# Shifted ranks, a planned transfer queue and another order at the end, in a kernel whose order a planner writes

## The chip, the cores and the metric

The kernel runs on one core of a Trainium2 chip. A core has five engines that run their own instruction lists and meet through semaphores: TensorE (PE, matrix products; its weight loads are listed as PEld), VectorE (DVE), ScalarE (ACT), GpSimd (POOL) and SyncE (SP), which here does nothing but issue transfers (DMAs). SBUF is the on-chip memory; PSUM, in eight banks of 128 partitions x 512 floats, takes the results of TensorE. The metric is the time of one execution in microseconds (us) on the device, as the median of several runs; lower is better.

## What is computed

Two attention layers over 2048 tokens of width 512, side by side in one output. Cut to what matters:

```python
def A(x, wq, wk, wv, wo):                      # 32 query heads of 16, one shared key/value head
    q = heads(x @ wq); k = x @ wk; v = x @ wv
    p = softmax(einsum("bhqd,bkd->bhqk", q, k) / 4)
    return merge(einsum("bhqk,bkd->bhqd", p, v)) @ wo

def B(x, wqkv, w_phi, wo):                     # linear attention with a feature map
    q, k, v = heads(x @ wqkv)
    phi = lambda t: concat(softmax(t @ w_phi), softmax(-(t @ w_phi)))
    kv = einsum("bhsf,bhsd->bhfd", phi(k), v); z = phi(k).sum(over tokens)
    return merge(phi(q) @ kv / (phi(q) @ z + 1e-6)) @ wo

return concat([A(...), B(...)], axis=-1)
```

Nearly all work is in A: 32 heads x 2048 x 2048 exponentials, 134 million. B needs no pairwise scores.

## The kernel before, in words

**Units.** The scores of A are cut into 32 stages (`sc`; 512 queries of one group of four heads), each of 16 quads (one key block of 128 by the four heads of a group), each quad of four units: one matrix product with 32 rows of contraction (L1611) that fills one PSUM bank with 128 x 512 scores. That makes 512 quads and 2048 units.

**Two ways to an exponential.** Most quads go to ScalarE: `next_qk` gathers three units and then two, in turn, into banks 0 to 2 and 3 to 4, and `expo` (L1672) takes the exponential of all of them in one instruction into the ring `PT` of 20 slots. The others go to VectorE: `next_dq` puts one unit at a time into a free bank, `bits` (L1782) turns scores into half-precision bit patterns by one multiply and add with integer output, and after four units `shift` (L1795) makes three shifted copies; TensorE adds up the four copies with fitting weights (L1828), which gives a close approximation of the exponential. A quad on VectorE takes four L1782 and three L1795. Which quad goes where isn't fixed: VectorE takes one whenever the planner finds it free enough (`dq_ok`, `dve_quad`).

**Sums.** The exponentials times the values, and the row sums beside them, accumulate in bank 5 (`ACC`), by L1726 for quads from ScalarE and L1828 for those from VectorE. When all 16 quads of a stage are in, `finish_sc` copies the bank out (`accS`, L1426), and the row sums go a long way: a transfer lays them out over partitions (`denC`, L1852, four transfers), VectorE takes reciprocals (L1860), four transfers bring them back to a row (L1865) and four spread the row over 16 partitions (`denS`, L1871), and `finish_sc3` multiplies (L1878). Odd stages are written to `Od` and moved into `On` by four more transfers (L1884). After every eight stages `outproj` makes four output blocks, copied to `outA` (ring of two) and stored (L1907). In the last stage the row sums have a bank of their own (`den_bank`), filled in the same steps as `ACC`, and `finish_last` computes reciprocals on ScalarE as exp(-ln) (L1926, L1928), multiplies on VectorE (L1932), adds the last quarter of the output projection (L1936) to what `out_part` (L1917, jobs `pp`) has put into four banks, copies (L1944 and L1426) and stores (L1946): blocks 0 and 2 issued by ScalarE, blocks 1 and 3 by SyncE. Part B's work is woven in between (`jobs_b`): projections L2042, L2072 and L2133, exponentials L2050 and L2140, products L2150 and L2186, and VectorE work on them.

**The planner.** None of this order is written out. Each piece is a job with an engine, an assumed duration, the jobs it comes after, the number of PSUM banks it needs (0 to 4 belong to ScalarE's scores, 6 and 7 are the free ones) and a rank, `prio`, where less is sooner. `run` plays the machine forward in a model of its own time: for every engine it lists the jobs that may start, keeps those within 0.02 us of the earliest, takes the one with the least `rank`, and issues it. The order in which jobs are issued is the order of the instruction lists that the engines get; on the chip each engine follows its list and waits on semaphores. `tr` and `tw` hold when the model thinks a tile was last read and written. A batch of transfers (`dmas`) is given a fixed time from its producer's end to its landing, whatever else stands on SyncE.

**Fillers.** TensorE's clock is kept up with products that add zero (`fill`, L1420, and `company`, L1403). `put_fill` and `short` place them where the planner reckons too little activity; they need a bank: `ACC` while a stage is open, otherwise a free one, otherwise the first bank of the next scores.

## Time and profile before

| | us |
|---|---|
| median of 3 runs (lowest, highest) | 769.65 (767.93, 771.23) |
| the profiled execution | 767.89 |
| its span, first to last instruction | 765.8 |
| ScalarE busy | 742.8 (97%) |
| PE busy | 716.3 (94%) |
| VectorE busy | 712.0 (93%) |
| mean granted clock of TensorE | 0.995 of full |

Rows of groups read: line, engine, operation, output<-inputs, shapes, count | busy us, mean ns of one | idle time of the engine before them and what ended it. Rows of a timeline: start, duration, engine, line, operation, tiles, count, and in brackets the idle time before. SPq and ACTq are the sequencers of SyncE and ScalarE issuing transfers. Rows of stretches: from:to, length, busy time of each engine with its count of instructions, granted clock, share of the transfer engines, GB/s. Busy time of ScalarE and VectorE counts the union of overlapping instructions, so a pause shorter than the overlap isn't seen in it.

Of the kernel before, what the change touches and what calls it, by code (L numbers as in the profile page):

```python
# [1169 lines left out]
class _Fast:  # L1170
# [16 lines left out]
    def __init__(self, nc, st, ins, out):  # L1187
# [75 lines left out]
        self.last_full = 0.0  # L1263

# [246 lines left out]
    def jobs_a(self):  # L1511
        ps, xT, job = self.ps, self.xT, self.job
# [200 lines left out]
    def pv(self, q):  # L1713

        ps, PT, VA = self.ps, self.PT, self.VA
        sc, kap = self.aquads[q]
        slots = [(4 * q + g) % self.RING for g in range(4)]
        todo = [(self.ACC, VA[:, sc % 2, kap, :], self.sums(sc))]
        if sc == 31:
            d = self.dens()  # L1720
            todo.append((self.den_bank, self.ones[:, 0:32], d))
        for bank, w, (start, stop) in todo:
            def fn(pe, bank=bank, w=w, start=start, stop=stop):
                mm = None
                for g in range(4):
                    mm = pe.matmul(ps[32 * g:32 * g + 32, bank, :], lhsT=w, rhs=PT[:, slots[g], :], start=start, stop=stop, tile_position=(0, 32 * g))  # L1726
# [115 lines left out]
    def finish_sc(self, sc):  # L1842

        ps = self.ps
        r = sc % 2
        accS, denC = self.accS, self.denC
        self.copy(accS[:, r, :], ps[:, self.ACC, :], [("PS", self.ACC)], [("accS", r)])
        fs = []
        for g in range(4):
            src = accS[32 * g + 16 - 16 * r:32 * g + 17 - 16 * r, r, :].rearrange("p (b c) -> p b c", b=32)  # L1850
            dst = denC[32 * g:32 * g + 32, r, :]
            fs.append((lambda s_, d_: (lambda q: q.dma_start(d_, s_)))(src, dst))  # L1852
        self.dmas(fs, [("accS", r)], [("denC", r)], 4.4)
        if self.rec is None:
            self.acc_sc = sc + 1

    def finish_sc2(self, sc):
        r = sc % 2
        denC, R = self.denC, self.denS
        self.add("dve", lambda v: v.reciprocal(out=denC[:, r, :], in_=denC[:, r, :]), reads=[("denC", r)], writes=[("denR", r), ("denC", r)])  # L1860
        fs = []
# [4 lines left out]
        self.dmas(fs, [("denR", r)], [("row", r), ("denS", r)], 4.4)  # L1866
# [5 lines left out]
        self.dmas(fs, [("row", r)], [("denS", r)], 11.0)  # L1872

    def finish_sc3(self, sc):
# [5 lines left out]
        if r:  # L1880
# [4 lines left out]
            self.dmas(fs, [key], [("On", sl)], 5.0)  # L1885
# [15 lines left out]
    def outproj2(self, qt):  # L1901
# [5 lines left out]
        self.dmas([lambda q: q.dma_start(dst, oa[:, ring, :])], [("outA", ring)], [], 4.0, is_output=True)  # L1907


    def out_part(self, i):  # L1910
        ps, On = self.ps, self.On
        bank = self.bank(("pp", i))

        def fn(pe):
            mm = None
            for A in range(4):
                mm = pe.matmul(ps[:, bank, :], lhsT=On[:, A, i * 128:i * 128 + 128], rhs=self.wo2[:, A, :], start=(A == 0), stop=False)  # L1917
            return mm
        self.add("pe", fn, reads=[("On", A) for A in range(4)] + ["wo2"], writes=[("PS", bank)])

    def finish_last(self):
# [8 lines left out]
        for h in range(2):  # L1930
# [3 lines left out]
            for i in range(2 * h, 2 * h + 2):  # L1934
                bank = self.bank(("pp", i))
                self.add("pe", (lambda i, bank: (lambda pe: pe.matmul(ps[:, bank, :], lhsT=Od[:, 1, i * 128:i * 128 + 128], rhs=self.wo2[:, 3, :], start=False, stop=True)))(i, bank),  # L1936
                         reads=[("Onl", h), "wo2"], accum=[("PS", bank)])
        for i in range(4):
            bank = self.bank(("pp", i))
# [5 lines left out]
            dst = self.out[0, (12 + i) * 128:(13 + i) * 128, 0:512]  # L1945
            self.S.dma1((lambda o, dst: (lambda q: q.dma_start(dst, o)))(o, dst), reads=[key], queue="sp" if i % 2 else "act", is_output=True)  # L1946

    def flag_calc(self):
# [7 lines left out]
        self.dmas([lambda q: q.dma_start(self.mrow, mqk)], [("mqk", k) for k in range(4)], ["mrow", "Bwv"], 8.0)  # L1956
# [273 lines left out]
    def b_s8c(self, st):  # L2230
# [3 lines left out]
        self.dmas([lambda e: e.dma_start(dst, ob[:, st % 3, :])], [("outB", st % 3)], [], 4.0, is_output=True)  # L2234
# [11 lines left out]
    FORCE = 3.3  # L2246
    LAST = 6
# [22 lines left out]
    def run(self):  # L2270
        while True:
            picks = []
            for eng, c in self.cand.items():
# [11 lines left out]
                now = [o for o in opts if o[0] <= lo + 0.02]  # L2285
# [7 lines left out]
            bank = self.ACC if self.open else next((b for b in self.free if self.tr.get(("PS", b), (0.0,))[0] + self.SEM <= self.te["pe"]), None)  # L2293
# [21 lines left out]
    def put_fill(self, n, m, bank, te):  # L2315
        cols = [512] * (n // 4) + ([128 * (n % 4)] if n % 4 else [])
        start = bank != self.ACC
# [11 lines left out]

    def rank(self, o):  # L2330

        s, j = o
        p = j.prio
        if j.eng == "pe":
# [95 lines left out]
```

### The profile page before, as it was taken

The numbers are of one execution on the slowest core, as the hardware profiler recorded it, in microseconds if no ns is written. First come the engines' busy times: TensorE is split into PE (matmuls) and PEld (weight loads), VectorE is DVE, ScalarE is ACT, GpSimd is POOL, SyncE is SP. The second block draws the span as 40 slices with busy tenths as digits, with TensorE's granted clock in tenths as the row PEclk, the third lists the DMA queues.
The fourth block names the chain that finished last, engine by engine and source line by source line (L and its number), as shares of the span: only waits on it lengthen the run. The fifth ranks groups of instructions, "written<-read, shape, count | busy, mean of one in ns | idle before, by whom it ended". The sixth has DMA issues, their size and how long they took to land.

```text
span 765.8 us, 17760 instructions
## 1 busy us (share of the span) xinstructions
PE 716.3 (94%) x7536; PEld 240.5 (31%) x7596; DVE 712.0 (93%) x1242; ACT 742.8 (97%) x694; POOL 18.5 (2%) x73
## 2 busy tenths in 40 slices
PE   7999999999998999999999999999999999999997
PEld 3332333233332333333332332223333333333222
DVE  3999999999998998799999999999997999999991
ACT  5999999999999999999999999999998999999996
POOL 6000000000000002000000000000000000000000
PEclk9999999999999999999999999999998999999999
DMA  9911011111012101110111110112111011111102
GB/s 183 206 9 8 6 8 13 8 10 12 1 12 36 9 6 8 13 9 16 19 9 19 16 15 14 15 11 30 22 20 8 20 28 25 23 15 12 10 8 38
DMA packets 47521, 18.15 MB, mean 24 GB/s; under 512 B 38468, under 2 KB 45572, under 8 KB 47432
## 3 DMA queue, kind: packets, MB, share of 16 engines
q1 hardware_dynamic: 44920, 16.47, 16.6%
q8 instruction: 61, 1.00, 0.5%
q10 hardware_dynamic: 2512, 0.44, 0.4%
q14 instruction: 28, 0.23, 0.1%
HBM read 2.15 MB, written 4.19 MB: 8 GB/s over the span
## 4 chain that ended last, share of the span: by engine, by line
ACT 73%; DVE 12%; PE 11%; DMA 2%; SPq 1%; issue 0%; ACTq 0%
ACT f_PT L1672 70%; DVE f_Z L1782 4%; PE f_ps L1611 3%; DVE f_Z L1795 3%; PE f_ps L1828 2%; ACT f_ET L2140 2%; PE f_ps L1726 2%; ACT f_Ek L2050 1%; DVE f_ssum L2056 1%; DMA f_AxT<-in_A_x_dram 1%; DVE f_vS L2082 1%; DVE f_Wk L2196 1%; PE f_ps L1420 1%; PE f_ps L1403 0%; PE f_ps L1917 0%
## 5 line engine op out<-in xcount | busy, mean ns | idle before, releaser
L1672 ACT ACTIVATE f_PT<-f_ps 128x1536 bf16<-128x1536 f32 x623 | 716.3, 1311 | 14.9 <-DVE f_VK L1581 8.2
L1782 DVE TENSOR_SCALAR f_Z<-f_ps 128x512 int16<-128x512 f32 x492 | 320.7, 680 | 17.4 <-PE f_ps L1611 15.8
L1611 PE MATMUL f_ps<-f_QA,f_KR 32*128 32x512 bf16 x2048 | 314.7, 385 | 23.2 <-ACT f_PT L1672 11.2
L1795 DVE TENSOR_SCALAR f_Z<-f_Z 128x2048 int16<-128x2048 int16 x369 | 243.0, 684 | 0.4
L1611 PEld LDWEIGHTS f_ps<-f_QA,f_KR 32*128 32x128 bf16 x2048 | 81.7, 91 | 237.7 <-ACT f_PT L1672 134.5
L1726 PE MATMUL f_ps<-f_PT,f_VA 128*32 128x512 bf16 x1556 | 153.5, 391 | 2.2 <-DVE f_accS L1426 1.8
L1828 PE MATMUL f_ps<-f_Z,f_VK 128*32 128x512 f16 x1968 | 129.5, 383 | 1.1 <-DVE f_accS L1426 0.4
L1726 PEld LDWEIGHTS f_ps<-f_PT,f_VA 128*32 128x32 bf16 x1556 | 38.7, 93 | 98.9 <-issue 88.3
L1420 PE MATMUL f_ps<-f_ones,f_zero 128*128 128x512 bf16 (+10 forms) x372 | 66.2, 345 | 3.0 <-POOL f_zero L1438 1.3
L1828 PEld LDWEIGHTS f_ps<-f_Z,f_VK 128*32 128x32 bf16 x1968 | 42.4, 96 | 56.9 <-issue 12.6
L1403 PE MATMUL f_ps<-f_ones,f_zero 32*128 32x512 bf16 x144 | 49.4, 380 | 0.3
L1420 PEld LDWEIGHTS f_ps<-f_ones,f_zero 128*32 128x32 bf16 (+2 forms) x372 | 19.1, 97 | 32.7 <-issue 21.9
L2196 DVE TENSOR_TENSOR f_Wk<-f_ps,f_wq 128x512 bf16<-128x512 f32 x32 | 21.8, 683 | 0.0
L1426 DVE COPY f_accS<-f_ps 128x512 f32<-128x512 f32 x31 | 21.3, 686 | 0.1
L2140 ACT ACTIVATE f_ET<-f_ps 128x512 bf16<-128x512 f32 x32 | 20.1, 772 | 0.0
L2082 DVE TENSOR_TENSOR f_vS<-f_ps,f_rs 128x1024 bf16<-128x1024 f32 x16 | 19.5, 1219 | 0.0
L2056 DVE TENSOR_REDUCE f_ssum<-f_Ek 128x64 f32<-128x1024 bf16 x16 | 19.3, 1208 | 0.1
L2050 ACT ACTIVATE f_Ek<-f_ps 128x512 bf16<-128x512 f32 x32 | 19.3, 721 | 0.0
L2072 PE MATMUL f_ps<-f_Bwv,f_BxT 128*128 128x512 bf16 x53 | 14.3, 380 | 2.8 <-DVE f_outA L1426 1.2
L2133 PE MATMUL f_ps<-f_BxT,f_Wq 128*128 128x512 bf16 x54 | 14.5, 380 | 2.0 <-issue 1.2
L2042 PE MATMUL f_ps<-f_Wk,f_BxT 128*128 128x512 bf16 x57 | 15.0, 381 | 1.4 <-issue 0.6
L1403 PEld LDWEIGHTS f_ps<-f_ones,f_zero 32*128 32x128 bf16 x144 | 11.4, 92 | 15.1 <-issue 11.4
(100 smaller groups left out, 320.6 us busy)
## 6 DMA issues: line engine op xcount, KB each, us to landing
f_denS<-f_denS SPq DMA_DIRECT2D x124, 30.0 KB, 3.1
out_dram<-f_outB SPq DMA_DIRECT2D x16, 128.0 KB, 2.7
f_denC<-f_accS SPq DMA_DIRECT2D x124, 2.0 KB, 1.7
f_denS<-f_denC SPq DMA_DIRECT2D x124, 2.0 KB, 1.7
out_dram<-f_outA SPq DMA_DIRECT2D x14, 128.0 KB, 2.1
f_On<-f_Od SPq DMA_DIRECT2D x60, 16.0 KB, 1.8
f_Bwv<-in_B_wqkv_dram SPq DMA_DIRECT2D x1, 512.0 KB, 4.7
f_Bwo<-in_B_wo_dram SPq DMA_DIRECT2D x1, 512.0 KB, 5.3
```

The lines of the kernel that those rows point to most:

```text
L1403: self.add("pe", lambda pe: pe.matmul(out, lhsT=zero[0:32, :], rhs=rhs, start=False, stop=False, tile_position=(0, 0)), reads=["ones", "ze ...
L1420: mm = pe.matmul(ps[x:x + m, bank, 0:n].rearrange("p (a n) -> p a n", n=128), lhsT=zero[0:r, 0:m], rhs=rhs, start=start, stop=start, **kw)
L1611: return pe.matmul(self.ps[:, bank, :], lhsT=self.KR[32 * g:32 * g + 32, sc % 2, kap * 128:(kap + 1) * 128], rhs=self.QA[32 * g:32 * g + 3 ...
L1672: self.add("act", lambda a: a.activation(out=PT[:, sl[0]:sl[0] + size, :], in_=ps[:, b0:b0 + size, :], func=ACT.Exp), reads=[("PS", b0 + i ...
L1726: mm = pe.matmul(ps[32 * g:32 * g + 32, bank, :], lhsT=w, rhs=PT[:, slots[g], :], start=start, stop=stop, tile_position=(0, 32 * g))
L1782: self.add("dve", lambda v: v.tensor_scalar(out=o, in0=ps[:, bank, :], scalar1=self.Z1, scalar2=self.Z0, op0=ALU.mult, op1=ALU.add), reads ...
L1795: self.add("dve", lambda v: v.tensor_scalar(out=Z[:, t], in0=Z[:, 0], scalar1=256.0 * t, scalar2=None, op0=ALU.add), reads=zk, writes=[("Z ...
L1828: mm = pe.matmul(ps[32 * g:32 * g + 32, bank, :], lhsT=w[:, k, :], rhs=Zf[:, k, sl[g], :], start=start and k == 0, stop=stop and k == 3, t ...
L2050: self.add("act", (lambda a, sg: (lambda e: e.activation(out=Ek[:, r, a].rearrange("p h f -> p (h f)"), in_=ps[:, bank, :], func=ACT.Exp, ...
L2082: self.add("dve", lambda v: v.tensor_tensor(out=vS[:, :, :, 0:16], in0=v3, in1=rs.unsqueeze(3).to_broadcast([128, 2, 32, 16]), op=ALU.mult ...
L2140: self.add("act", lambda e: e.activation(out=self.ET[:, sl, :], in_=self.ps[:, bank, :], func=ACT.Exp, scale=sg), reads=[("PS", bank)], wr ...
L2196: self.add("dve", lambda v: v.tensor_tensor(out=o, in0=i, in1=w.unsqueeze(3).to_broadcast([128, 16, 2, 16]), op=ALU.mult), reads=[("PS", b ...
```

## The change

Three things are changed, and none of the arithmetic.

1. *Ranks.* The model's time is cut into stretches of 20 us. Each has a number in `SEEDS` (38 numbers, ten of them 0). Where it isn't 0, every job's rank is shifted by up to half a unit either way, by a checksum of the number and the job's name, and the number modulo 4 chooses how late a job may start and still compete (0.02, 0.02, 0.06 or 0.12 us).
2. *Transfers.* `dmas` models SyncE as one queue (`spq`): a batch starts when the queue has come free, its producer has ended and what it reads has landed, takes 0.64 us per transfer, and lands a given time later. The given times are smaller than before in exchange. Fillers may also use `ACC` between two stages.
3. *The end.* `out_part` is cut into four jobs of one product each, ranked behind the sums, and the first of them may start while the last exponentials run, once the row sums of the last stage have their bank, only one free bank is left and part B needs none. In the last stage `den_bank` is filled before `ACC`. All four last stores are issued by SyncE, after all four copies.

```diff
@@ dmas
+        self.spq = max([self.spq, self.fin + 0.05] + [self.tw[r][0] + 0.1 for r in reads if r in self.tw]) + 0.64 * len(fs)
+        end = self.spq + us
         for r in reads:
-            self.tr[r] = max(self.tr.get(r, (0.0, "sp")), (self.fin + us, "sp"))
+            self.tr[r] = max(self.tr.get(r, (0.0, "sp")), (end, "sp"))
         for w in writes:
-            self.tw[w] = (self.fin + us, "sp")
+            self.tw[w] = (end, "sp")
@@ jobs_a
-            job(("pp", i), "pe", 0.87, (lambda i: (lambda: self.out_part(i)))(i), mode="full", nb=1, prio=2.0, ok=lambda: self.ended,
-                after=[("on", 24 + a) for a in range(7)])
+            for A in range(4):
+                job(("pp", i, A), "pe", 0.22, (lambda i, A: (lambda: self.out_part(i, A)))(i, A), mode="full", nb=0 if A else 1, prio=4.0,
+                    ok=lambda: self.asc >= 32 and self.dn % 4 == 0 and (self.ended or (self.den_bank is not None and len(self.free) == 1 and not self.rest_b())),
+                    after=[("pp", i, A - 1)] if A else [("on", 24 + a) for a in range(7)])
@@ pv
-        for bank, w, (start, stop) in todo:
+        for bank, w, (start, stop) in todo[::-1]:
@@ finish_sc, finish_sc2, finish_sc3, outproj2, b_s8c: landing times
-        self.dmas(fs, [("accS", r)], [("denC", r)], 4.4)
+        self.dmas(fs, [("accS", r)], [("denC", r)], 1.8)
-        self.dmas(fs, [("denR", r)], [("row", r), ("denS", r)], 4.4)
+        self.dmas(fs, [("denR", r)], [("row", r), ("denS", r)], 1.8)
-        self.dmas(fs, [("row", r)], [("denS", r)], 11.0)
+        self.dmas(fs, [("row", r)], [("denS", r)], 4.0)
-            self.dmas(fs, [key], [("On", sl)], 5.0)
+            self.dmas(fs, [key], [("On", sl)], 1.9)
-        self.dmas([lambda q: q.dma_start(dst, oa[:, ring, :])], [("outA", ring)], [], 4.0, is_output=True)
+        self.dmas([lambda q: q.dma_start(dst, oa[:, ring, :])], [("outA", ring)], [], 2.0, is_output=True)
...
@@ out_part
-    def out_part(self, i):
+    def rest_b(self):
+        return any(j.nb and j.name[0] not in ("pp", "dq") for c in (self.cand["pe"], [w for ws in self.waiting.values() for w in ws]) for j in c)
+
+    def out_part(self, i, A):
...
+        kw = dict(accum=[("PS", bank)]) if A else dict(writes=[("PS", bank)])
+        self.add("pe", lambda pe: pe.matmul(ps[:, bank, :], lhsT=On[:, A, i * 128:i * 128 + 128], rhs=self.wo2[:, A, :], start=(A == 0), stop=False),
+                 reads=[("On", A), "wo2"], **kw)
@@ finish_last
-            self.S.dma1((lambda o, dst: (lambda q: q.dma_start(dst, o)))(o, dst), reads=[key], queue="sp" if i % 2 else "act", is_output=True)
+            outs.append((o, key, self.out[0, (12 + i) * 128:(13 + i) * 128, 0:512]))
+        for i in (0, 1, 2, 3):
+            o, key, dst = outs[i]
+            self.S.dma1((lambda o, dst: (lambda q: q.dma_start(dst, o)))(o, dst), reads=[key], is_output=True)
@@ class constants
+    SEG = 20.0
+    JITTER = 1.0
+    SEEDS = (596854, 729634, 32076, 399722, 242082, 0, 0, 0, 0, 323517, 1029782, 888628, 860342,
+             597688, 434556, 856097, 34036, 281692, 360021, 0, 0, 231316, 0, 984916, 944571, 0,
+             641864, 18972, 805256, 0, 267693, 1039384, 154486, 560249, 867978, 713965, 845664, 0)
@@ run
-                now = [o for o in opts if o[0] <= lo + 0.02]
+                seed = self.seed(lo)
+                now = [o for o in opts if o[0] <= lo + (0.02, 0.02, 0.06, 0.12)[seed % 4]]
...
-            bank = self.ACC if self.open else next((b for b in self.free if self.tr.get(("PS", b), (0.0,))[0] + self.SEM <= self.te["pe"]), None)
+            bank = self.ACC if self.open else next((b for b in self.free + ([self.ACC] if self.acc_sc is not None and self.ndone[self.acc_sc] == 0 else [])
+                                                    if self.tr.get(("PS", b), (0.0,))[0] + self.SEM <= self.te["pe"]), None)
@@ rank
+        seed = self.seed(s)
+        if seed:
+            p += self.JITTER * (zlib.crc32(("%d%s" % (seed, j.name)).encode()) / 4294967296.0 - 0.5)
```

More of the change, by code (lines that the diff above doesn't have):

```diff
@@ L1 @@
+import zlib
 import contextlib
@@ L1263, in __init__ @@
         self.last_full = 0.0
+        self.spq = 30.0
     TAIL = dict(pe=0.17, act=0.15, dve=0.085, pool=0.1)
@@ L2316, in put_fill @@
         cols = [512] * (n // 4) + ([128 * (n % 4)] if n % 4 else [])
-        start = bank != self.ACC
+        start = bank != self.ACC or not self.open
         self.issue(_Job(("fill", len(self.log)), "pe", 0.0533 * n, lambda: self.fill(cols, start=start, mode=m, bank=bank), (), m, 0, (), 0, 9, None), te)
@@ L2328, in short, with seed @@
         return a + own < self.FORCE
+    def seed(self, t):
+        i = int(t / self.SEG)
+        return self.SEEDS[i] if i < len(self.SEEDS) else 0
     def rank(self, o):
```

18 lines of the change are left out of this document (6 added, 12 removed).

## The prediction

> **What bounds the kernel now.** I read the page first: busy time of each engine, then the costliest groups.
>
> ```profile
> span 765.8 us, 17760 instructions
> PE 716.3 (94%) x7536; PEld 240.5 (31%) x7596; DVE 712.0 (93%) x1242; ACT 742.8 (97%) x694; POOL 18.5 (2%) x73
> ...
> ACT 73%; DVE 12%; PE 11%; DMA 2%; SPq 1%; issue 0%; ACTq 0%
> ...
> L1672 ACT ACTIVATE f_PT<-f_ps 128x1536 bf16<-128x1536 f32 x623 | 716.3, 1311 | 14.9 <-DVE f_VK L1581 8.2
> L1782 DVE TENSOR_SCALAR f_Z<-f_ps 128x512 int16<-128x512 f32 x492 | 320.7, 680 | 17.4 <-PE f_ps L1611 15.8
> L1795 DVE TENSOR_SCALAR f_Z<-f_Z 128x2048 int16<-128x2048 int16 x369 | 243.0, 684 | 0.4
> L1726 PE MATMUL f_ps<-f_PT,f_VA 128*32 128x512 bf16 x1556 | 153.5, 391 | 2.2 <-DVE f_accS L1426 1.8
> ```
>
> ScalarE is the bound, with the chain of waits lying on its exponential (L1672) for most of the span; VectorE is almost as full. The two share one pool of work. There are 2048 score units of 512 columns; VectorE takes 492 of them (L1782) in groups of four, 123 quads, and ScalarE the other 1556 (the count of L1726). So an idle microsecond on either engine is worth something: on ScalarE directly, on VectorE if the planner fills it with a quad. By these rows a quad costs VectorE 4 x 320.7/492 + 3 x 243.0/369 = 4.58 us, and takes 4 x 716.3/1556 = 1.84 us off ScalarE. That ratio, 0.40 us of ScalarE for one of VectorE, prices most of what follows.
>
> Next I cut the span into stretches, to see where either engine is idle.
>
> ```profile
> core 0: us, PE busy (x) PEld busy (x) DVE busy (x) ACT busy (x) POOL busy (x), PEclk, DMA share, GB/s
> 20.00:240.00 220.00, 207.31 (x2223) 67.98 (x2240) 217.78 (x379) 219.84 (x210) 1.18 (x5) 1.00 0.18 25
> 240.00:254.00 14.00, 11.26 (x118) 3.51 (x119) 10.53 (x18) 11.71 (x11) 0.00 (x0) 1.00 0.20 43
> 254.00:580.00 326.00, 307.21 (x3266) 106.20 (x3296) 313.69 (x541) 325.52 (x310) 4.20 (x10) 1.00 0.13 15
> 580.00:592.00 12.00, 11.80 (x123) 3.85 (x127) 7.71 (x16) 8.92 (x8) 0.00 (x0) 0.72 0.12 8
> 592.00:736.00 144.00, 138.22 (x1400) 45.01 (x1399) 141.90 (x245) 143.45 (x128) 0.00 (x0) 1.00 0.15 19
> 736.00:756.00 20.00, 19.61 (x250) 5.69 (x248) 9.74 (x20) 19.73 (x19) 0.00 (x0) 1.00 0.14 12
> 756.00:766.00 10.00, 4.82 (x27) 1.71 (x26) 2.26 (x4) 2.68 (x6) 0.00 (x0) 0.98 0.17 57
> ...
> 300.00:320.00 20.00, 18.96 (x194) 6.67 (x196) 14.38 (x27) 20.00 (x23) 2.62 (x7) 1.00 0.12 8
> 500.00:520.00 20.00, 18.91 (x175) 6.23 (x177) 17.87 (x31) 20.00 (x22) 0.00 (x0) 1.00 0.13 17
> ```
>
> In the three quiet stretches, 690 us together, ScalarE is idle only 0.16 + 0.48 + 0.55 = 1.19 us and VectorE 2.22 + 12.31 + 2.10 = 16.63. Two holes stand out: at 240 to 254 ScalarE loses 2.29 us and VectorE 3.47, at 580 to 592 they lose 3.08 and 4.29. From 756 the tail runs off with every engine mostly idle. So the change has five places to pay in, and nothing of tens of microseconds.
>
> **Term 1, the transfer queue in the plan (the hole at 240).** Timelines of SyncE, VectorE and ScalarE:
>
> ```profile
> 237.08 3.35 SPq L1871 DMA_DIRECT2D f_denS<-f_denS  x4
> 240.47 6.23 SPq L1907 DMA_DIRECT2D out_dram<-f_outA  x4
> 243.28 0.69 DVE L1426 CAST f_outA<-f_ps 128x512 bf16<-128x512 f32 x1 [3.58 <-DMA out_dram<-f_outA]
> 245.43 1.02 ACT L1672 ACTIVATE f_PT<-f_ps 128x1024 bf16<-128x1024 f32 x1 [0.79 <-PE f_ps L1611]
> ```
>
> An output store stood on SyncE behind four spreads of the reciprocals, so its buffer came free late; VectorE stood 3.58 us before the copy that needed the buffer, and behind that copy the banks, the scores and the exponential went dry. The old plan gave each batch a fixed time from its producer; the new one gives 0.64 us per transfer on one queue, behind earlier batches, plus a landing time. For a batch met alone the sums are the old ones (4 x 0.64 + 1.8 = 4.36 against 4.4), so only collisions like this one change, and here VectorE would get other work first. No device wait is added. I take ScalarE's whole 2.29 us: **-2.3** (ends 0 and -3.6, VectorE's own wait). What is late next is the store itself, which nobody reads.
>
> **Term 2, the halved clock (the hole at 580).**
>
> ```profile
> 578.00:581.40 3.40, 2.43 (x21) 0.72 (x17) 3.40 (x7) 2.92 (x4) 0.00 (x0) 0.99 0.02 1
> 581.40:588.20 6.80, 6.71 (x57) 1.88 (x57) 3.90 (x8) 4.42 (x4) 0.00 (x0) 0.50 0.03 4
> 579.53 0.84 PE L1420 MATMUL f_ps<-f_ones,f_zero 128*128 128x512 bf16 x2 [0.79 <-ACT f_PT L1672]
> ```
>
> TensorE was busy 2.43 of 3.40 us, then got half the clock for 6.8 us; this is the one such event between start and tail. The filler at L1420 that should keep TensorE active waited 0.79 us for a bank that ScalarE still read. The change lets fillers use the accumulator bank between two stages once it has been copied out, and every changed rank rearranges the order. Each event is a coincidence of this order; with one in 745 us, none is about as likely as one, and the extra bank tips it. I take the hole as gone: **-3.1** (ends 0 and -3.4, half of 6.8). If an event stays, this term and its share of term 3 go.
>
> The Trainium skill ("TensorE: Matmul & The Clock Gate", section "HAM oscillation — how this bites in real kernels") gives as its abstract rule no gaps of TensorE over about 3.4 us. The rows above differ: the clock fell after a gap of 0.79 us. By that rule fillers that come a little sooner would be beside the point, and with term 2 and its share of term 3 at nothing the sum would be -7.2 instead of -12.0.
>
> **Term 3, quads for the VectorE time that terms 1 and 2 free.** 3.47 + 4.29 = 7.76 us, over 4.58, is 1.69 quads; times 1.84: **-3.1** (ends 0, if nothing is taken up, and -3.7 for two whole quads).
>
> **Term 4, the shifted ranks.** Every job's rank moves by up to half a unit, in 28 of 38 stretches of 20 us, and jobs up to 0.12 us later compete. Ten entries are 0 and leave the order alone. Host arithmetic costs the chip nothing. The trace can't show the new order, so bounds. Gain: all 16.63 us of quiet VectorE idle becomes quads, 3.63 x 1.84 = 6.7. Loss: the mean of quiet idle is 0.48 us in 20; if every shifted stretch became like 500 to 520 (2.13), 28 x 1.65 = 46 us, 10 quads, +18.5. Between these I go by one stretch, 300 to 320, with 5.62 us of the idle:
>
> ```profile
> 303.29 1.04 PE L2133 MATMUL f_ps<-f_BxT,f_Wq 128*128 128x512 bf16 x4 [0.26 <-ACT f_ET L2140]
> 310.33 0.69 DVE L1782 TENSOR_SCALAR f_Z<-f_ps 128x512 int16<-128x512 f32 x1 [1.87 <-PE f_ps L1611]
> ```
>
> VectorE waits there for scores (L1611) from a TensorE that runs full-size projections (L2133), and the ranks among just those jobs are what is shifted. I take that stretch mended and the rest as it is, 5.62/4.58 x 1.84 = 2.26: **-2.2**.
>
> **Term 5, the end.** Timelines of TensorE, ScalarE, VectorE and the queues:
>
> ```profile
> 755.90 0.81 PE L1917 MATMUL f_ps<-f_wo,f_On 128*128 128x512 bf16 x3 [0.16 <-issue]
> 756.64 0.40 PE L1726 MATMUL f_ps<-f_PT,f_VA 128*32 128x512 bf16 x4
> 756.87 0.39 PE L1726 MATMUL f_ps<-f_PT,f_ones 128*32 128x512 bf16 x4
> 757.19 2.76 PE L1917 MATMUL f_ps<-f_wo,f_On 128*128 128x512 bf16 x12
> 757.31 0.38 ACT L1926 ACTIVATE f_ET<-f_ps 128x256 f32<-128x256 f32 x1 [1.48 <-PE f_ps L1726]
> 758.17 0.48 DVE L1932 SCALAR_TENSOR_TENSOR f_Od<-f_ps,f_odd,f_ET 128x256 bf16<-128x256 f32 x1 [6.67 <-ACT f_ET L1928]
> 759.79 1.03 PE L1936 MATMUL f_ps<-f_wo,f_Od 128*128 128x512 bf16 x4
> 760.90 0.38 ACTq L1946 DMA_DIRECT2D out_dram<-f_outB  x1
> 761.22 2.36 SPq L1946 DMA_DIRECT2D out_dram<-f_outA  x2
> 761.38 0.60 ACT L1944 ACTIVATE f_outB<-f_ps 128x512 bf16<-128x512 f32 x1 [0.51 <-ACT f_outB L1944]
> 233.50 2.44 SPq L1865 DMA_DIRECT2D f_denS<-f_denC  x4
> ```
>
> The last sums (L1726) wait behind a projection of four matmuls; cut into single ones with a lower rank, they let the sums go 0.7 us sooner, and with the denominators' bank first another 0.2 (756.87 against 756.64): the logarithm starts 0.9 us earlier. The last projections (L1936) also wait for the twelve matmuls of L1917, until 759.79, though their first input is there at 758.65. One of the four banks may now be filled while the last exponentials run; the other three still go in the last two microseconds. So L1936 starts at best 0.9 us before 758.65, at 757.75, which is 2.0 before 759.79; the logarithm's 0.9 alone is the lower end of the gain. Against it: four stores on SyncE instead of two. At 0.61 us each (2.44 over 4) the last store may stand one issue longer, up to +0.6; in return ScalarE's second copy no longer waits 0.51 behind ScalarE's own store. Store 3 now stands behind store 2 and so behind ScalarE's second copy, which ends before VectorE's. I take **-1.3** (ends +0.6 and -2.0).
>
> **The sum.** -2.3 - 3.1 - 3.1 - 2.2 - 1.3 = -12.0 us. The profiled execution took 767.89 us, its span 765.8 and 2.1 around it; it becomes 755.9. The median of the runs, 769.65, is 1.76 above it, so I predict **757.6**.
>
> **Rivals.**
> - *The clock halves once in the new order as well.* For it: TensorE was busy for 2.43 of 3.40 us before the event, no rare thing once the order is another; against it the other 745 us of this order. Price: term 2 and the 4.29 us in term 3, 4.29 x 0.40 = 1.7: 757.6 + 3.1 + 1.7 = **762.4**. The Trainium skill's rule on gaps, above, leads to the same time.
> - *The gain is much larger*: all quiet VectorE idle goes. For it: 254 to 580 has 12.31 us of it in a few lumps. Against: VectorE also needs free banks and TensorE. 757.6 - 6.7 + 2.2 = **753.1**, and with the far ends of terms 1, 2, 3 and 5 another 2.9: 750.2.
> - *The plan moves and the chip doesn't*: holes of the old size open elsewhere, and term 4 is nothing; only term 5 is left: **768.4**. For it: unloaded transfers are priced as before.
> - *Slower, by starved VectorE*: shifted ranks put full-size projections ahead of VectorE's scores, as at 300 to 320. Each such stretch costs 5.62 less 0.48, 5.14 x 0.40 = 2.1 us. Without term 4 the sum is -9.8; it comes out 0.5% slower (+3.85) from 13.65/2.1, seven such stretches of 28; with eight: 769.65 - 9.8 + 16.8 = **776.7**. Against it: in before there is one in 35 quiet ones.
>
> **Chances.** My forecast 0.43 (753 to 761), larger gain 0.15, clock event 0.20, only the end 0.12, starved 0.10. The first three are faster by over 0.5%, about what a measurement here can tell from no change (3.85 us): 0.78; the fourth within: 0.12; the last slower: 0.10. Range 750 to 769: from the larger gain's far end to past the case with only the end; left out are the starved case and little more.
>
> **What would show it.** Term 1: no VectorE wait on an output store above 1 us. Term 2: clock 1.00 in every stretch between 20 and 750. Terms 3 and 4: L1782 counts 492 + 4 x (1.7 + 1.2), about 504, and L1726 about 1544; VectorE idle in the quiet part under 12 us. Term 5: the logarithm (L1926) starts within 0.7 us of the last exponential's end, against 1.5. The prediction is wrong if L1782's count falls, if a clock of 0.50 shows more than once, or if a new wait on transfers takes the hole's place.

## The result, and the profile after

The changed kernel takes 759.15 us in the median (757.53 to 761.31, 4 runs), the one before 770.44 in the runs beside it (767.93 to 771.62); the ratio on record is 0.9875, with a 95% interval of 0.9847 to 0.9903 (the plain medians give 0.985). The forecast was 757.6 against 769.65. The time came out as forecast; the reasons, as the experiments show, mostly did not.

The page of the kernel after, its busy times and costliest groups (line numbers have moved: L1672 is now L1678, L1611 L1617, L1782 L1788, L1795 L1801, L1726 L1732):

```profile
span 758.6 us, 17911 instructions
PE 717.7 (95%) x7636; PEld 238.7 (31%) x7636; DVE 716.4 (94%) x1249; ACT 739.3 (97%) x692; POOL 19.8 (3%) x73
...
L1678 ACT ACTIVATE f_PT<-f_ps 128x1536 bf16<-128x1536 f32 (+1 forms) x621 | 711.6, 1327 | 9.6 <-PE f_ps L1617 8.9
...
L1788 DVE TENSOR_SCALAR f_Z<-f_ps 128x512 int16<-128x512 f32 x496 | 322.5, 679 | 11.4 <-PE f_ps L1617 8.4
...
L1732 PE MATMUL f_ps<-f_PT,f_VA 128*32 128x512 bf16 x1552 | 151.5, 388 | 0.8 <-ACT f_PT L1678 0.2
```

VectorE took one quad more (496 units, not 492), not the three that I had reckoned with. Its idle time before L1788 fell from 17.4 us to 11.4. The view of stretches, of after and then of before, cut at the last stage:

```profile
20.00:729.00 709.00, 677.70 (x7230) 224.81 (x7222) 697.35 (x1207) 708.00 (x662) 6.63 (x15) 1.00 0.15 19
729.00:749.00 20.00, 19.94 (x267) 6.39 (x265) 8.38 (x15) 18.53 (x20) 0.00 (x0) 1.00 0.14 10
749.00:759.00 10.00, 2.67 (x11) 0.86 (x11) 1.88 (x4) 1.40 (x3) 0.00 (x0) 0.86 0.18 57
```

```profile
20.00:736.00 716.00, 675.80 (x7118) 226.55 (x7174) 691.60 (x1195) 709.43 (x662) 5.38 (x15) 1.00 0.15 19
```

Between 20 us and the last stage ScalarE is idle 1.00 us instead of 6.57, and VectorE 11.65 instead of 24.40; in this execution both holes are gone and no new one has come, and the clock is 1.00 throughout. What I had not expected stands in the end. Its timelines, after:

```profile
745.19 1.94 ACT L1678 ACTIVATE f_PT<-f_ps 128x1024 bf16<-128x1024 f32 x2 [0.75 <-PE f_ps L1617]
747.76 0.38 ACT L1931 ACTIVATE f_ET<-f_ps 128x256 f32<-128x256 f32 x1 [0.63 <-PE f_ps L1732]
747.85 3.01 PE L1923 MATMUL f_ps<-f_wo,f_On 128*128 128x512 bf16 x11
748.62 0.49 DVE L1937 SCALAR_TENSOR_TENSOR f_Od<-f_ps,f_odd,f_ET 128x256 bf16<-128x256 f32 x1 [5.78 <-ACT f_ET L1933]
750.71 1.03 PE L1941 MATMUL f_ps<-f_wo,f_Od 128*128 128x512 bf16 x4
751.34 1.29 DVE L1430 CAST f_outA<-f_ps 128x512 bf16<-128x512 f32 x2 [1.51 <-PE f_ps L1941]
751.81 0.35 SPq L1954 DMA_DIRECT2D out_dram<-f_outB  x1
752.27 1.39 SPq L1954 DMA_DIRECT2D out_dram<-f_outA  x1
753.75 0.38 SPq L1954 DMA_DIRECT2D out_dram<-f_outB  x1
754.18 0.44 SPq L1954 DMA_DIRECT2D out_dram<-f_outA  x1
```

The last exponential ends at 747.13, 8.7 us sooner than before (755.83), but from there to the span's end it takes 11.5 us instead of 10.0. The logarithm starts 0.63 us after the exponential instead of 1.48, as forecast. Eleven of the sixteen products L1923 still stand between it and L1941, though, and the four stores leave SyncE one behind the other, the second taking 1.39 us to issue.

**How times are compared below.** Runs of one kernel differ by up to 11 us, and nearly all of that goes with the granted clock, which each run reports. I put one straight line through 114 runs of all kernels here, with a level of its own for each kernel. By it a run takes 0.59 us more (plus or minus 0.04) for each 0.001 of mean clock that is missing, with 0.67 us of scatter left. Two runs that are listed as slow stand outside the line, the table and the ratios: 770.26 us of `after_again` and 770.52 us of `no_acc_fill`, its profiled one, both at a clock of 0.980. The level at a clock of 1.000 is called the time at full clock: it holds the order's own holes, and the rest is half-speed time. The clock's shortfall times 590 us gives that rest, roughly: shortfall at the very end, when TensorE has no work left, costs nothing, and in the profiled execution of `after` all of its 0.0016 lies behind 756.2 us.

```
kernel          runs  median   at full clock   mean (1 - clock)   L1788 (or its like): count, idle before it
before            42  768.34   765.0 +- 0.3    0.0062             492, 17.4
after              4  759.15   757.8 +- 0.7    0.0025             496, 11.4
after_again        6  761.08   758.4 +- 0.6    0.0052             the same order
queue_only         5  773.85   766.6 +- 0.8    0.0112             492, 25.2
no_shift           6  774.55   768.2 +- 0.7    0.0103             492, 24.1
other_numbers      4  777.99   771.1 +- 0.8    0.0108             476, 28.8
shift_only         4  778.99   773.8 +- 0.8    0.0093             480, 37.3
half_numbers       6  762.98   760.8 +- 0.6    0.0048             496, 15.9
no_acc_fill        3  758.80   757.8 +- 0.8    0.0030             as after but for seven fillers
end_only          10  768.53   765.6 +- 0.5    0.0064             492, 17.0
old_end            5  758.82   757.7 +- 0.6    0.0022             496, 11.6
stores_act         5  761.07   759.3 +- 0.7    0.0038             the order of after
stores_two         5  758.31   757.6 +- 0.6    0.0012             the order of after
fill_more          9  762.75   761.8 +- 0.5    0.0038             496, 12.3
```

### The profile page after: what moved, and what is told of

Read it like the earlier page. It is cut to its first block, busy times and chain, and to the rows that moved or that the text cites. A ratio compares the mean times of both kernels' runs of the same rounds, so it can differ in the third digit from the quotient of the medians.

```text
span 758.6 us, 17911 instructions
## 1 busy us (share of the span) xinstructions
PE 717.7 (95%) x7636; PEld 238.7 (31%) x7636; DVE 716.4 (94%) x1249; ACT 739.3 (97%) x692; POOL 19.8 (3%) x73
## 4 chain that ended last, share of the span: by engine, by line
ACT 71%; DVE 15%; PE 12%; DMA 1%; issue 0%; DVEq 0%
ACT f_PT L1678 67%; DVE f_Z L1788 7%; DVE f_Z L1801 5%; PE f_ps L1617 4%; PE f_ps L1834 3%; PE f_ps L1732 2%; ACT f_Ek L2058 2%; ACT f_ET L2148 1%; DMA f_AxT<-in_A_x_dram 1%; PE f_ps L1407 1%; PE f_ps L1923 1%; PE f_ps L1424 1%; DVE f_outA L1430 0%; DVE f_outB L1430 0%; PE f_ps L2141 0%
## 5 line engine op out<-in xcount | busy, mean ns | idle before, releaser
L1678 ACT ACTIVATE f_PT<-f_ps 128x1536 bf16<-128x1536 f32 (+1 forms) x621 | 711.6, 1327 | 9.6 <-PE f_ps L1617 8.9
L1617 PE MATMUL f_ps<-f_QA,f_KR 32*128 32x512 bf16 x2048 | 309.3, 384 | 27.2 <-ACT f_PT L1678 15.2
L1788 DVE TENSOR_SCALAR f_Z<-f_ps 128x512 int16<-128x512 f32 x496 | 322.5, 679 | 11.4 <-PE f_ps L1617 8.4
L1801 DVE TENSOR_SCALAR f_Z<-f_Z 128x2048 int16<-128x2048 int16 x372 | 244.2, 680 | 0.4
L1617 PEld LDWEIGHTS f_ps<-f_QA,f_KR 32*128 32x128 bf16 x2048 | 79.5, 91 | 241.4 <-ACT f_PT L1678 139.7
L1732 PE MATMUL f_ps<-f_PT,f_VA 128*32 128x512 bf16 x1552 | 151.5, 388 | 0.8 <-ACT f_PT L1678 0.2
L1424 PE MATMUL f_ps<-f_ones,f_zero 128*32 128x512 bf16 (+10 forms) x408 | 69.6, 346 | 2.0 <-POOL f_zero L1442 1.3
L1732 PEld LDWEIGHTS f_ps<-f_PT,f_VA 128*32 128x32 bf16 x1552 | 38.3, 93 | 93.2 <-issue 83.4
L1407 PE MATMUL f_ps<-f_ones,f_zero 32*128 32x512 bf16 x136 | 46.9, 379 | 0.2
L1430 DVE CAST f_QA<-f_ps 128x512 bf16<-128x512 f32 x16 | 10.9, 682 | 7.6 <-PE f_ps L1607 7.6
L1607 PE MATMUL f_ps<-f_AxT,f_wq 128*128 128x512 bf16 x64 | 16.6, 381 | 0.8 <-DMA f_AxT<-in_A_x_dram 0.7
L2234 PE MATMUL f_ps<-f_Bwo,f_oT 128*128 128x512 bf16 x64 | 16.6, 382 | 0.1
L2080 PE MATMUL f_ps<-f_Bwv,f_BxT 128*128 128x512 bf16 x64 | 16.6, 381 | 0.1
```

The source lines that it names most:

```text
L1407: self.add("pe", lambda pe: pe.matmul(out, lhsT=zero[0:32, :], rhs=rhs, start=False, stop=False, tile_position=(0, 0)), reads=["ones", "ze ...
L1424: mm = pe.matmul(ps[x:x + m, bank, 0:n].rearrange("p (a n) -> p a n", n=128), lhsT=zero[0:r, 0:m], rhs=rhs, start=start, stop=start, **kw)
L1430: self.add("dve", lambda v: v.tensor_copy(out=out, in_=in_), reads=reads, writes=writes)
L1617: return pe.matmul(self.ps[:, bank, :], lhsT=self.KR[32 * g:32 * g + 32, sc % 2, kap * 128:(kap + 1) * 128], rhs=self.QA[32 * g:32 * g + 3 ...
L1678: self.add("act", lambda a: a.activation(out=PT[:, sl[0]:sl[0] + size, :], in_=ps[:, b0:b0 + size, :], func=ACT.Exp), reads=[("PS", b0 + i ...
L1788: self.add("dve", lambda v: v.tensor_scalar(out=o, in0=ps[:, bank, :], scalar1=self.Z1, scalar2=self.Z0, op0=ALU.mult, op1=ALU.add), reads ...
```

## The experiments

**The table of numbers emptied.** `no_shift`, on the changed kernel:

```diff
-    SEEDS = (596854, 729634, 32076, ... 713965, 845664, 0)
+    SEEDS = (0,) * 38
```

> The changed kernel with every number in the table 0: the queue in the plan, the fillers and the end stay, no rank is shifted. My theory (terms 1 to 3 carry the gain, the shift only 2.2 us): about 761.5 us, VectorE with 495 or 496 of L1788, and no hole by a store behind the spreads. Rival (the chosen numbers carry it): 766 to 770 us, L1788 at 492 or less, holes of other kinds. A single half-speed stretch of the clock adds about 4 us to either and shows in the granted clock.

Measured: 774.55 us, 1.0072 of before (1.0044 to 1.0100). So everything that my terms 1, 2, 3 and 5 speak of, without the shift, makes the kernel slower, and the table is worth 768.2 - 757.8 = 10.4 us at full clock beside the half-speed time. This row of its page, the twin of the one above, shows what gets worse:

```profile
L1788 DVE TENSOR_SCALAR f_Z<-f_ps 128x512 int16<-128x512 f32 x492 | 322.3, 682 | 24.1 <-PE f_ps L1617 19.2
```

VectorE is idle for 24.1 us before L1788, 19.2 of them waiting for scores (L1617) from TensorE. No quad is taken more than before.

**Other numbers of the same kind.** `other_numbers`, on the changed kernel: each number that isn't 0 is raised by 4, which keeps its tolerance and changes its checksums.

```diff
-    SEEDS = (596854, 729634, 32076, ...
+    SEEDS = (596858, 729638, 32080, ...
```

> The changed kernel with each number that isn't 0 raised by 4: the same tolerance for each stretch, as much shift, another checksum. If any shift of this size does (my theory puts the gain in the queue and the quads, whatever the order): 757 to 763 us. If these very numbers carry the gain: worse than with no shift at all, 765 to 775 us, with VectorE idle in new places (L1788 at 488 or less).

Measured: 777.99 us, 1.0116 (1.0079 to 1.0154), worse than no shift at all, with five quads fewer than after:

```profile
L1788 DVE TENSOR_SCALAR f_Z<-f_ps 128x512 int16<-128x512 f32 x476 | 310.3, 682 | 28.8 <-PE f_ps L1617 24.2
```

This other table costs time, 771.1 against 768.2 at full clock, where the first one gains 10.4 us. So the first one's numbers look fitted to this plan, as far as one other table can tell. This is the rival of the starved VectorE, which I had given 0.10: it describes the shift by that other table. (A half-speed stretch of 17.07 us, from 24 us on, adds to the idle time in this execution; the line takes it out of the level at full clock.)

**The queue alone.** `queue_only`, on the kernel before: `dmas` and the landing times as in the change, nothing else.

```diff
+        self.spq = max([self.spq, self.fin + 0.05] + [self.tw[r][0] + 0.1 for r in reads if r in self.tw]) + 0.64 * len(fs)
+        end = self.spq + us
```

> The kernel before, with the transfers planned as a queue and nothing else. My theory: the hole at 240 goes (2.3 us of ScalarE and 1.4 for its VectorE time), 766 us without a half-speed stretch of the clock, 770 with one; no VectorE wait on an output store over 1 us. Rival (the new order opens holes of the old size elsewhere): 769 to 771 us with another VectorE wait on a transfer of 2 us or more.

Measured: 773.85 us, 1.0047 (1.0003 to 1.0092). VectorE's waits, longest first:

```profile
DVE f_Z L1785 <- PE f_ps L1614: 20.2, 26, 2.1
DVE f_KR L1558 <- PE f_ps L1550: 10.0, 4, 6.0
DVE f_Od L1935 <- ACT f_ET L1931: 6.5, 2, 6.4
DVE f_QA L1429 <- PE f_ps L1604: 5.0, 2, 3.0
```

The waits on an output store (3.6 us before) and on the spread reciprocals (4.5) are gone: the queue in the plan does what it says. The time isn't gained. VectorE now waits 20.2 us for scores from TensorE instead of 15.8, and the profiled execution has three half-speed stretches of 6.8 us and one of 3.4; the 3.0 us for `QA` (563.7 to 566.7) lie inside one of them (562.3 to 569.1).

**The other end alone.** `end_only`, on the kernel before: the three edits of the end (single products behind the sums, denominators first, four stores on SyncE).

> The kernel before, with the other order at the end and nothing else (single products, denominators first, all stores on SyncE). Everything up to about 735 us should be as before. As predicted, 1.3 us faster: 768.5. By the trace of the changed kernel, where the time from the last exponential to the end grew from 10.0 to 11.5 us: 1.5 us slower, 771.5 us.

Measured: 768.53 us, 1.0021 (0.9996 to 1.0045). At full clock 765.6 against 765.0: no gain, and at most a small loss. Its timeline shows why, beside the lines of before in the prediction (L1919 is their L1917, L1937 their L1936):

```profile
756.76 0.38 ACT L1927 ACTIVATE f_ET<-f_ps 128x256 f32<-128x256 f32 x1 [0.94 <-PE f_ps L1728]
756.86 3.90 PE L1919 MATMUL f_ps<-f_wo,f_On 128*128 128x512 bf16 x14
760.59 1.03 PE L1937 MATMUL f_ps<-f_wo,f_Od 128*128 128x512 bf16 x4
```

The logarithm starts 0.55 us sooner than in before, but the last projections start 0.80 us later (760.59 against 759.79): fourteen single products now stand ahead of them and take 0.28 us each, where twelve in whole projections took 0.23 each.

This run shows something else. Its order up to the end is that of before. The view of stretches, of this kernel and then of before:

```profile
55.00:70.00 15.00, 14.22 (x114) 3.95 (x113) 12.32 (x22) 12.30 (x12) 0.00 (x0) 0.77 0.01 1
578.00:592.00 14.00, 12.96 (x157) 4.81 (x157) 12.29 (x24) 13.15 (x12) 0.00 (x0) 1.00 0.02 3
```

```profile
55.00:70.00 15.00, 13.91 (x142) 4.47 (x142) 14.39 (x26) 14.88 (x15) 0.00 (x0) 1.00 0.02 2
578.00:592.00 14.00, 12.95 (x131) 4.11 (x131) 9.71 (x20) 10.92 (x10) 0.00 (x0) 0.76 0.10 7
```

The same order was halved at 581 us in one execution and at 59 us in the other, each time for 6.83 us, and not at the other's place. ScalarE lost 2.6 us more there (14.88 less 12.30) or 2.2 (13.15 less 10.92). So the hole that I read at 580 had two parts. About 0.9 us is the order's; the rest is a matter of one execution, and other executions have it elsewhere or not at all.

**The changed kernel again**, as a reference for the next runs, and **the last stores issued by ScalarE**, or **two stores instead of four**:

```diff
-            self.S.dma1((lambda o, dst: (lambda q: q.dma_start(dst, o)))(o, dst), reads=[key], is_output=True)
+            self.S.dma1((lambda o, dst: (lambda q: q.dma_start(dst, o)))(o, dst), reads=[key], queue="act", is_output=True)
```

```diff
-        for i in (0, 1, 2, 3):
...
+        dst = self.out[0, 1536:2048, 0:512].rearrange("(t u p) n -> u p t n", t=2, u=2)
+        self.S.dma1(lambda q: q.dma_start(dst[0], self.outB[:, 0:2, :]), reads=[("outB", 0), ("outB", 1)], queue="act", is_output=True)
+        self.S.dma1(lambda q: q.dma_start(dst[1], oa[:, 0:2, :]), reads=[("outA", 0), ("outA", 1)], is_output=True)
```

> The changed kernel itself, as the reference for the runs beside it, and for how often its clock is halved. Theory from the runs so far: about 757.8 us at a granted clock of 1.000, and some 0.6 us more for each 0.001 of clock below.

> The changed kernel with all four last stores issued by ScalarE, after both of its copies, and none by SyncE. Theory: the end grew because four stores stand in a row on SyncE, the second of which took 1.39 us to issue, so the last left at 754.2 though its copy was done at 752.6; on ScalarE, at 0.38 us an issue, it leaves by 753.9 or sooner: 1 to 2 us faster than the changed kernel. Rival (the wait for the last product and the landing set the end, not the issue): no difference.

> The changed kernel with two last stores of twice the size instead of four: ScalarE's two blocks in one, issued by ScalarE, VectorE's two in one, issued by SyncE. Theory of the row of issues: the last leaves by 753.0 at the latest, lands 2.5 to 3 us after, 1.5 to 2.5 us faster than the changed kernel. Rival as for the other: no difference.

Measured, with the ratio to before: the changed kernel 0.9908 (0.9871 to 0.9945), all on ScalarE 0.9910 (0.9878 to 0.9943), two stores 0.9864 (0.9839 to 0.9890). At full clock 758.4, 759.3 and 757.6, each known to about 0.6: ScalarE is no better than SyncE, and two stores are at best a little better than four. The four stores of the changed kernel by SyncE took 2.8 us of the 11.5 (751.81 to 754.62); on ScalarE the second of them stalled in the same way (0.98 us), so that run hardly shortened the row and settles nothing. Two stores do shorten it: the last is issued at 752.40 instead of 754.18, and the expected 1.5 to 2.5 us aren't seen in the times. So the row of issues isn't what sets the end. The packets of the profiled executions show what comes behind:

```
                 data packets of the last stores     16 KB packet of the instruction queue   last store issued, landed
after            752.65-755.66, nine at 756.98-757.67     755.91-756.99                      754.18, 758.13
after_again      752.40-755.16, nine at 756.63-757.27     755.15-756.64                      753.71, 757.74
stores_act       753.05-755.61, nine at 756.82-757.45     755.54-756.82                      754.10, 757.91
stores_two       752.90-754.62                            754.64-755.91                      752.40, 754.95
end_only         762.53-765.34                            765.33-766.52                      763.82, 765.69
no_acc_fill      764.99-767.85                            767.84-768.94                      766.31, 768.24
```

In the first three, nine data packets (one sixteenth of a store) come only when a 16 KB instruction packet ends, and the last store lands 3.8 to 4.0 us after its issue; in the other three all data are through as that packet begins, and it lands after 1.9 to 2.6 us. That fits data packets queued behind an instruction packet on one of the 16 transfer engines. No run here changed the instruction packet itself, so this reading is argued and not shown. What is shown is that one and the same order takes 11.5 us from the last exponential to the end in `after` and 9.3 in `no_acc_fill`, so the growth from 10.0 to 11.5 us isn't in the order. Two runs of `after` have spans of 755.7 and 756.2 us, which leaves no room for 11.5 us behind a last exponential at 746.8 to 747.5 (five profiled executions), so it seems to differ from execution to execution. With two stores the spans of the five runs are 756.4 to 756.9. But the best runs of the changed kernel, which has the same order, are as good (757.53 and 758.11 us against 758.13), so it isn't shown to beat it.

**Half of the numbers.** `half_numbers`: the first 19 kept, the last 19 set to 0.

> The changed kernel with the first 19 numbers kept and the last 19 set to 0: the order up to 380 us of the planner's time is the changed kernel's, from there ranks aren't shifted. If each number is fitted to the order that the numbers before it leave, the gain stops there or is given back in part: 762 to 768 us at full clock. If the second half would go as well unshifted: within 2 us of the changed kernel.

Measured: 762.98 us, 0.9932 (0.9899 to 0.9966), 760.8 at full clock. The times by which so many of the 2048 units were done, from one profiled execution each, less those of before (a unit is done when its exponential on ScalarE ends, or the third shift of its quad on VectorE):

```
units done    before    queue_only  no_shift   after   half_numbers  other_numbers  shift_only
150            64.2       -0.6        +0.5      +0.5      +0.6          +8.5          +0.4
450           177.2       -0.6        +2.6      -0.4      -0.2          +5.3          -0.5
1150          441.7       +2.0        +3.6      -7.7      -7.5          +7.8          +7.1
1750          656.7       +7.2        +6.2     -11.5      -7.7          +6.2          +5.5
2048          755.8       +7.1        +6.5      -8.7      -5.0          +8.7         +10.3
```

Half-speed stretches are in these times: most of the 8.5 us of `other_numbers` at 150 units is the stretch of 17.07 us from 24 us on. Up to 1150 units the half table keeps step with the full one, then it falls 3.7 us behind, 2 or 3 of them in a half-speed stretch of 6.83 us at 527. At full clock the half table keeps 7.4 of the 10.4 us that the full one gains over `no_shift` (768.2 - 760.8), and 4.2 of the 7.2 over before (765.0 - 760.8); the second half adds 3.0 to it. So both halves of the table earn a part. Both forecasts miss: it gave back less than 762 to 768 at full clock, and more than the 2 us of the other. The table of units can't tell in which stretch the gain is made, since part B's work stands in other places in each order.

**The numbers without the rest**, and **the fillers without the extra bank.** `shift_only` puts `SEEDS`, `rank` and the tolerance into the kernel before; `no_acc_fill` takes one clause from the changed one:

```diff
-            bank = self.ACC if self.open else next((b for b in self.free + ([self.ACC] if self.acc_sc is not None and self.ndone[self.acc_sc] == 0 else [])
+            bank = self.ACC if self.open else next((b for b in self.free
```

> The kernel before with the same 38 numbers and tolerances, but without the transfer queue, the extra bank for fillers and the other end. If the numbers fit only the exact plan that they were found for: like the run with other numbers, 770 to 779 us, VectorE with fewer L1788 than 492. If these ranks are good in themselves: 757 to 763 us.

> The changed kernel without the accumulator bank for fillers between stages. In the instruction list only a handful of fillers go, all else keeps its place. My term 2 (the extra bank keeps the clock up): more half-speed stretches, 2 to 4 us slower than the changed kernel in the median. Rival (too few fillers to matter; whether the clock halves is decided by how a run falls): the time of the changed kernel, 757.9 us at full clock, and as wide a spread.

Measured: 778.99 us, 1.0139 (1.0083 to 1.0194), for the numbers on the old plan, the slowest of all:

```profile
L1783 DVE TENSOR_SCALAR f_Z<-f_ps 128x512 int16<-128x512 f32 x480 | 313.4, 681 | 37.3 <-PE f_ps L1612 33.2
```

The same 38 numbers that gain 10.4 us on the new plan lose 8.8 on the old one. Of the two plans they fit one. Without the extra bank: 0.9877 (0.9820 to 0.9933), 757.8 at full clock, the changed kernel's time. By the traces the clause takes out three fillers and lengthens four, all but one of them before 14 us, and nothing else moves. Whether the bank keeps half-speed stretches away is left open: one run of four without it was at a clock of 0.980, with stretches of 17.07, 6.83 and 6.83 us, and so was one of seven of `after_again`, which has it. `other_numbers`, with the bank, was halved for 17.07 us at 24.1 us, where `no_acc_fill` was at 24.3.

**The old end on the changed kernel**, and **longer fillers**: `old_end` undoes the three edits of the end; `fill_more` is the kernel with two stores, and each filler gets 256 columns more, which the plan isn't told.

```diff
-        cols = [512] * (n // 4) + ([128 * (n % 4)] if n % 4 else [])
+        m2 = n + 2
+        cols = [512] * (m2 // 4) + ([128 * (m2 % 4)] if m2 % 4 else [])
```

> The changed kernel with the end of the kernel before: whole projections of four products ranked ahead of the sums, values' sums before denominators, stores 0 and 2 by ScalarE, 1 and 3 by SyncE. If the new end is worth the 1.3 us that I gave it: 759 us at full clock. By the trial of the new end on the kernel before (765.7 against 765.2 at full clock): no difference, 757.5 to 758 at full clock.

> The changed kernel with two stores at the end instead of four, and every filler half a product (256 columns) longer without the plan knowing of it, so the order is the same. If half-speed stretches follow TensorE's activity: none in any run, granted clock 0.998 or more throughout. The price is on TensorE, up to 0.1 us at each filler: if that is hidden, 757.7 us at full clock as with two stores; if not, up to 8 us more.

Measured: the old end 0.9872 (0.9828 to 0.9916), 757.7 at full clock. In the profiled executions the last unit is done at 747.1 us with either end, so the body is the same, and the new end is worth nothing (757.8 and 758.4 with it). Longer fillers: 0.9944 (0.9906 to 0.9981), 761.8 at full clock, so about 4 us of the price isn't hidden, and the clock still fell in some runs (0.983 in one of nine, 0.996 in two). With 0.0038 mean shortfall against 0.0012 to 0.0052 in the same order without them, this doesn't tell whether more activity of this kind helps the clock.

## Why the prediction was right, and where its steps were not

**The total** was right: 757.6 forecast, 759.15 measured, and the range held it. It was right by a sum of five terms of which none has the right size, and that they add up is luck. In one profiled execution each, the holes even closed as forecast: ScalarE's idle time fell by 5.57 us (6.57 to 1.00), where terms 1 and 2 together said 5.4. But the edits that were to close them don't do it by themselves. Most of the signs set out beforehand came true too (store waits, clock, VectorE's idle time under 12 us, the logarithm's start), so they could not tell this cause from another; the count of units on VectorE did not (496, forecast about 504).

**Term 1, the queue (-2.3).** Its mechanism is there: no wait on a store over 1 us is left, in the changed kernel or with the queue alone (one of 2.2 us on the spread reciprocals is still there in the changed kernel). What failed is "ScalarE's whole 2.29 us". With the queue alone the order loses 1.6 us at full clock (766.6 against 765.0) and gets more half-speed time. To take a wait out of a planned order makes another order, and its holes aren't those of the old one less one.

**Term 2, the clock (-3.1).** The event was read as "a coincidence of this order" that the extra bank tips. The bank isn't shown to do anything (`no_acc_fill`), and the same order is halved at 59 or at 581 us (`end_only` beside before). Of the six profiled executions that have the changed order to its last stage, all but a few fillers, five have no half-speed stretch ahead of the last products and one has 30.7 us of it (`no_acc_fill`). So an order has half-speed time only as an average over runs: 0.0062 of shortfall in 42 runs of before, 3.7 us by the line; 0.0031 in 28 runs of these six kernels, 1.8 us. With the two runs at 0.980 it is 0.0042 in 30, 2.5 us, and the difference to before is no longer clear. That is -1.2 to -1.8, and nothing shows that the bank makes it. The new plan without fitted numbers (`queue_only`, `no_shift`, `other_numbers`) and the table on the old plan have 0.009 to 0.011, 5 to 7 us. The Trainium skill, in "TensorE: Matmul & The Clock Gate", section "What's actually happening", says that the activity window runs free and doesn't start with the kernel. That agrees with one order halved at different places.

**Term 3, the quads (-3.1).** One quad was taken, not 1.7 with 1.2 more from term 4: -1.8. Between 20 us and the last stage the kernel is 7.0 us shorter (709 instead of 716); 5.57 of them are ScalarE's idle time, and 1.43 its busy time.

**Term 4, the shift (-2.2).** This is the step that failed in size, by far: the term was made from one stretch (300 to 320), and the table is worth 10.4 us at full clock against the same kernel without it. My bounds, -6.7 to +18.5, were counted from the order of before, but the table works on the order of the new plan, which is 3.2 us worse than before. Taken from before, all that the planner does in the changed kernel, terms 1 to 4, is worth 7.2 us at full clock and some 1 to 2 in clock. The trace of before could not tell whether the numbers were fitted, and I split the gain between mechanisms that could be read there.

**Term 5, the end (-1.3).** Nothing, by two runs (`old_end`, `end_only`). The step that the logarithm starts sooner came true (0.63 us against 1.48). The step that failed is the start of the last projections, put at 2.0 us sooner at best: counted from the last exponential's end they start 0.80 us later in `end_only` than in before (4.76 against 3.96), and on the changed body they start after 3.58 us with the new end and after 3.01 with the old one. Single products ranked behind the sums stand in a row ahead of them and take longer each, and that uses up what the logarithm gains. On the changed body eleven of the sixteen are left behind the sums, which is about what the prediction had said (three banks of four).

**The rivals.** The starved VectorE is real, for the one other table that was tried. The larger gain was nearer in mechanism: VectorE's idle time between 20 us and the last stage did halve (24.40 to 11.65 us), though only one quad came of it. The halved clock is no matter of one event in an order, but of runs.

## What to carry to other kernels

In an order that a planner writes, an edit to its model can change the whole order. Such an edit can't be priced by the hole that it closes: measure it alone, and beside a control that is as random as it is (the same numbers plus four). A table of fitted numbers belongs to the planner that it was found for: here the same numbers gained 10.4 us on one and lost 8.8 on the other. Where runs of one kernel spread by 1%, look at the granted clock of each run before you explain the spread by the code.

## What the runs showed of the hardware

The half-speed stretches come at places that differ between executions of the same order, in steps of 3.41 us (3.41, 6.83 and two of 17.07 us were seen). Some places come back in kernels of a like order: 610 and 743 us in both `queue_only` and `no_shift`, 24 us in both `other_numbers` and `no_acc_fill`. Over a span of some 765 us, 0.001 of mean clock is 1.5 us at half speed, and it costs 0.59, so a microsecond at half speed costs this kernel about 0.4.

Beyond that, the second of the stores that SyncE issued at the end took 0.95 to 1.79 us to issue in ten of eleven profiled executions, and 0.34 in `old_end`; the second on ScalarE took 0.98 us in a row of four and 0.37 in a row of two. All others took 0.34 to 0.59. In each of the long issues a 16 KB instruction packet had begun before it, and the issue ended 0.3 to 0.4 us after that packet did; in `old_end` the packet began later. The cause wasn't tried.
